# Linear attention block on one core: the five Wk blocks dealt out anew over the two DMA issue queues

## Chip, core and metric

The kernel runs on one core of a Trainium2 chip. The metric is the device time of one execution in microseconds (us); lower is better. The median of the four runs of the kernel before is the reference time.

## What is computed

`x` is [1, 2048, 640], `wqkv` is [640, 1920], `wo` is [640, 640], all bf16. The block is a linear attention with 32 heads of 20 columns:

```
q, k, v = split(x @ wqkv)                 # 3 x [2048, 640], 32 heads of 20
phi(t)  = where(t > 0, t + 1, exp(t)) + 1e-6
kv  = einsum("bhsd,bhse->bhde", phi(k), v)
z   = einsum("bhsd->bhd",       phi(k))
num = einsum("bhqd,bhde->bhqe", phi(q), kv)
den = einsum("bhqd,bhd->bhq",   phi(q), z) + 1e-6
out = (num / den) @ wo
```

## The kernel before, in words

The 2048 rows of `x` are cut into 16 tiles of 128 rows. The contraction over the 640 input columns is cut into five blocks of 128, so the weight for K, `Wk` (columns 640 to 1279 of `wqkv`), is loaded as five blocks of 128 x 640, called Wk blocks 0 to 4 here, 160 KB each.

The program is written as one list of operations for each engine. A helper, `Plan.add`, appends an operation to its engine's list and works out from the names it reads and writes which semaphores it must wait for. Nothing is reordered: the order in which `add` is called for an engine is the order in which that engine runs. A DMA is issued by the engine on whose list it stands. Two engines issue DMAs here, SyncE (SP) and ScalarE (ACT), and each has a queue of its own.

The start of the kernel is what matters for the change:

1. `load_wk` (L234) puts on the two queues the loads needed first: x tile 0 in two halves of 80 KB (L240, one half on each queue), x tile 1 (L229, on ACT) and the five Wk blocks (L249), dealt out by the two strings in L243. A string such as `w12` is Wk block 1, `x12` is x tile 1.
2. `load_xT` (L185) puts four transposing loads on SP (L187), which bring x tiles 2 to 15 straight into `xT`, transposed on the way by the DMA crossbar. They are called crossbar blocks 1 to 4 here and cover 2, 3, 4 and 5 tiles (256, 384, 512 and 640 rows).
3. `load_rest` (L257) puts the weights for Q and V, plain x tiles and `wo` on SP behind them.

TensorE (PE) begins with dummy matmuls (`warm`, L271). It transposes x tiles 0 and 1 itself (`transpose_x`, L197), as these come in plain form. DVE and ACT copy the two transposed tiles to `xT` (L211, L208). Then K is computed for tiles 0 and 1 block by block, in an order written out by hand, so that each Wk block is used as it lands:

```
order = "t1 k00 k10 k01 k11 k02 k12 k03 k13 k04 k14"
```

Here `k01` is the pair of matmuls (two column halves) of tile 0 with Wk block 1. That makes 20 matmuls at L281. Tiles 2 to 15 follow, 10 matmuls each; tile 2 is the first that needs crossbar block 1, tile 4 needs block 2, tile 7 block 3, tile 11 block 4. Each `k_half` waits for the Wk blocks and the part of `xT` that it reads. After K come the Q tiles (L334), the products of `phi(K)` with x (L308), the small products, the denominators and the output product (L514), interleaved by a second hand-written string; they all follow on PE in one fixed order.

Of the kernel before, what the change touches and what calls it, by code (L numbers as in the profile page):

```python
# [84 lines left out]
def bass_standalone__linear_attn_block__prompt_kernel(nc, x, wqkv, wo, out):  # L85
# [12 lines left out]
    with contextlib.ExitStack() as ctx:  # L98
# [129 lines left out]
        def load_xn(a, b, eng):  # L228
            P.add(eng, lambda e: e.dma_start(  # L229
                xn[:, a * D:b * D].rearrange("p (t n) -> p t n", n=D),  # L230
                x[0, 128 * a:128 * b, :].rearrange("(t p) n -> p t n", p=128)),
                writes=[("xn", t) for t in range(a, b)], dma=True)

        def load_wk():  # L234
            tl = mybir.InstLoadActFuncSet(
                name=nc.get_next_instruction_name(),
                act_func_set_id=ACT_TABLE_SET_LN_EXP, ins=[], outs=[])
            P.add("act", lambda e: e.add_instruction(tl), writes=["table"])
            for eng, lo in (("sp", 0), ("act", HALF)):
                P.add(eng, lambda e, lo=lo: e.dma_start(  # L240
                    xn[:, lo:lo + HALF], x[0, 0:128, lo:lo + HALF]),
                    writes=[("xn", 0, lo)], dma=True)
            for eng, what in (("sp", "w01 w23 w34"), ("act", "x12 w12 w45")):  # L243
                for k in what.split():
                    a, b = int(k[1]), int(k[2])
                    if k[0] == "x":
                        load_xn(a, b, eng)
                    else:
                        P.add(eng, lambda e, a=a, b=b: e.dma_start(  # L249
                            wk[:, a * D:b * D].rearrange("p (c n) -> p c n", n=D),  # L250
                            wqkv[128 * a:128 * b, D:2 * D].rearrange("(c p) n -> p c n", p=128)),
                            writes=[("wk", c) for c in range(a, b)], dma=True)
# [304 lines left out]

        pool_const()
        load_wk()
        load_xT()  # L560
        load_rest()
# [142 lines left out]
```

## Time and profile before

| what | value |
|---|---|
| median of 4 runs | 100.68 us (100.56 to 100.93) |
| the profiled execution: its own time | 100.75 us |
| the profiled execution: span of its instructions | 99.3 us |
| PE busy share of the span | 97% |
| DVE, ACT, POOL busy share | 64%, 45%, 5% |
| moved by DMA | 12.26 MB |
| share of 16 DMA engines, SP's queue (q1) and ACT's queue (q10) | 42.6% and 1.8% |

A line of the profile's groups reads: source line, engine, operation, out<-in by the program's names, shape, count; then busy us, mean ns of one, and the idle time of that engine just before them with what ended it. PE is the matmul, PEld the weight load that precedes each matmul, SPq and ACTq the instructions of the two issuing sequencers. "To landing" is counted from the start of the issuing instruction to the last of the DMA's completion signals. In the table by stretches of time, the DMA share is the mean busy share of the 16 DMA engines; it can be over 1 because packets overlap.

### The profile page before, as it was taken

How to read it: one execution, taken by the hardware profiler on the slowest of the kernel's cores; microseconds unless marked ns; L12 is line 12 of the kernel's file. 1: busy time of each engine (PE TensorE's matmuls, PEld its weight loads, DVE VectorE, ACT ScalarE, POOL GpSimd, SP SyncE). 2: the span in 40 equal slices, each digit the busy share in tenths (PEclk: the TensorE clock that was granted, in tenths of full speed). 3: DMA queues.
4: the chain of work that ended last, by engine and by line, in shares of the span. 5: the costliest groups of instructions: out<-in, count | busy, mean ns of one | idle time of the engine just before them, and what ended most of it. 6: DMA issues, size and time to landing. Idle time of an engine off the chain costs nothing.

```text
span 99.3 us, 1793 instructions
## 1 busy us (share of the span) xinstructions
PE 96.1 (97%) x694; PEld 65.0 (65%) x699; DVE 64.1 (64%) x133; ACT 45.2 (45%) x86; POOL 4.5 (5%) x17
## 2 busy tenths in 40 slices
PE   6999999999999999999999999999999999999992
PEld 2567777777756656655768868766556677777771
DVE  2104998888875999968895200669998409954332
ACT  5115455544524071066644364777855622333321
POOL 6300000000000000000002600000000000000000
DMA  1999999999997000000000024220220324273334
GB/s 46 303 266 217 230 195 193 369 374 363 362 243 149 0 0 0 0 3 3 0 7 0 0 61 115 57 65 0 81 63 0 131 60 116 103 255 107 132 132 132
DMA packets 18372, 12.26 MB, mean 123 GB/s; under 512 B 9917, under 2 KB 18365, under 8 KB 18365
## 3 DMA queue, kind: packets, MB, share of 16 engines
q1 hardware_dynamic: 17645, 11.55, 42.6%
q10 hardware_dynamic: 720, 0.61, 1.8%
q8 instruction: 5, 0.08, 0.3%
q14 instruction: 2, 0.02, 0.1%
HBM read 5.90 MB, written 2.62 MB: 86 GB/s over the span
## 4 chain that ended last, share of the span: by engine, by line
PE 96%; ACT 1%; issue 1%; DVE 0%
PE ps L281 22%; PE ps L514 22%; PE ps L334 21%; PE ps L308 18%; PE ps L621 4%; PE ps L271 3%; PE ps L445 2%; PE ps L424 1%; PE ps L197 1%; ACT w2g L464 1%; PE ps L482 1%; DVE osb L539 0%; PE ps L405 0%
## 5 line engine op out<-in xcount | busy, mean ns | idle before, releaser
L334 PE MATMUL ps<-xT,wqn 128*128 128x512 bf16 x95 | 22.6, 379 | 0.4 <-ACT w2g L464 0.2
L281 PE MATMUL ps<-wk,xT 128*128 128x320 bf16 x160 | 22.4, 303 | 0.0
L514 PE MATMUL ps<-w2p,pq 128*128 128x320 bf16 (+2 forms) x170 | 22.1, 291 | 0.0
L342 ACT ACTIVATE eq<-ps 128x512 bf16<-128x512 f32 x20 | 12.0, 598 | 18.6 <-PE ps L334 18.6
L514 PEld LDWEIGHTS ps<-w2p,pq 128*128 128x128 bf16 x170 | 15.9, 98 | 6.2 <-issue 0.2
L281 PEld LDWEIGHTS ps<-wk,xT 128*128 128x128 bf16 x160 | 15.8, 99 | 6.4 <-DMA wk<-in_wqkv_dram 0.3
L308 PE MATMUL ps<-pk,xn 128*128 128x360 bf16 (+1 forms) x130 | 19.1, 299 | 0.0
L334 PEld LDWEIGHTS ps<-xT,wqn 128*128 128x128 bf16 x100 | 11.6, 118 | 8.1 <-ACT w2g L464 0.2
L294 ACT ACTIVATE ek<-ps 128x640 bf16<-128x640 f32 x16 | 11.2, 704 | 11.3 <-PE ps L281 10.6
L308 PEld LDWEIGHTS ps<-pk,xn 128*128 128x128 bf16 x130 | 12.6, 98 | 5.6
L507 DVE TENSOR_TENSOR pq<-pq,rd 128x512 bf16<-128x512 bf16 x20 | 7.7, 419 | 10.7 <-PE ps L621 7.3
L299 DVE SCALAR_TENSOR_TENSOR pk<-ps,ek 128x640 bf16<-128x640 f32 x16 | 13.2, 825 | 0.6
L536 ACT CAST osb<-ps 128x320 bf16<-128x320 f32 (+1 forms) x17 | 7.0, 414 | 12.8 <-PE ps L514 9.4
L539 DVE CAST osb<-ps 128x320 bf16<-128x320 f32 (+2 forms) x17 | 7.7, 465 | 6.3 <-PE ps L514 6.3
L296 DVE TENSOR_SCALAR ek<-ek 128x640 bf16<-128x640 bf16 x16 | 5.2, 325 | 5.5 <-ACT ek L294 5.4
L355 DVE TENSOR_SCALAR eq<-eq 128x512 bf16<-128x512 bf16 x20 | 5.8, 288 | 2.2 <-ACT eq L342 2.1
L346 ACT ACTIVATE rq<-ps 128x512 bf16<-128x512 f32 x11 | 6.5, 591 | 0.0
L362 DVE SCALAR_TENSOR_TENSOR pq<-ps,eq 128x512 bf16<-128x512 f32 x9 | 6.2, 692 | 0.3
L368 DVE TENSOR_TENSOR za<-pk 128x1280 f32<-128x1280 bf16 x4 | 5.8, 1485 | 0.0
L359 DVE TENSOR_TENSOR pq<-eq,rq 128x512 bf16<-128x512 bf16 x11 | 4.7, 426 | 1.1 <-ACT rq L346 0.8
L621 PE MATMUL ps<-pk,xn 128*128 128x360 bf16 (+1 forms) x30 | 4.9, 299 | 0.0
L368 DVE TENSOR_TENSOR za<-za 128x1280 f32<-128x1280 f32 x3 | 4.5, 1484 | 0.0
(44 smaller groups left out, 43.3 us busy)
## 6 DMA issues: line engine op xcount, KB each, us to landing
out_dram<-osb SPq DMA_DIRECT2D x15, 160.0 KB, 1.8
xn<-in_x_dram SPq DMA_DIRECT2D x2, 640.0 KB, 9.5
xn<-in_x_dram SPq DMA_DIRECT2D x1, 960.0 KB, 7.7
wqn<-in_wqkv_dram SPq DMA_DIRECT2D x1, 800.0 KB, 5.6
wv<-in_wqkv_dram SPq DMA_DIRECT2D x1, 800.0 KB, 12.3
wog<-in_wo_dram SPq DMA_DIRECT2D x1, 750.0 KB, 13.2
w2p<-w2g SPq DMA_DIRECT2D x5, 150.0 KB
rd<-rdc SPq DMA_DIRECT2D x8, 64.0 KB, 2.2
```

The lines of the kernel that those rows point to most:

```text
L281: r = e.matmul(bank(b + h, HALF), xT[:, c * S + 128 * st:c * S + 128 * st + 128], wk[:, c * D + HALF * h:c * D + HALF * (h + 1)], start=(c ...
L294: P.add("act", lambda e: e.activation(fold(t[:, :]), two_banks(b), ACTF.Exp), reads=banks + ["table"], writes=[("ek", st % 3)])
L299: P.add("dve", lambda e: e.scalar_tensor_tensor(fold(pk[:, st * D:(st + 1) * D]), two_banks(b), 0.0, fold(t[:, :]), ALU.max, ALU.add), rea ...
L308: r = e.matmul(bank(d, PW[h]), xn[:, st * D + 128 * d:st * D + 128 * d + 128], pk[:, st * D + PO[h]:st * D + PO[h] + PW[h]], start=(st == ...
L334: r = e.matmul(bank(b), wqn[:, d * D:(d + 1) * D].rearrange("p (q c) -> p c q", c=NC_)[:, c, :], xT[:, d * S + BK * sbk:d * S + BK * (sbk ...
L342: P.add("act", lambda e: e.activation(t[:, :], bank(b), ACTF.Exp), reads=[("bank", b), "table"], writes=[("eq", i)])
L368: P.add("dve", lambda e: e.tensor_tensor(d_ap, a, b, ALU.add), reads=ra + rb, writes=[dst])
L507: P.add("dve", lambda e: e.tensor_tensor(v, v, rd[i][:, BK * h:BK * (h + 1)], ALU.mult), reads=[("rd", i, 2 * h), ("rd", i, 2 * h + 1), (" ...
L514: r = e.matmul(bank(b, hi - lo), pq[:, c * S + 128 * st:c * S + 128 * st + 128], w2p[:, c * D + lo:c * D + hi], start=(c == 0), stop=(c == ...
L536: P.add("act", lambda e: e.copy(osb[j][:, lo:hi], bank(b, hi - lo)), reads=[("bank", b)], writes=keys)
L539: P.add("dve", lambda e: e.tensor_copy(osb[j][:, lo:hi], bank(b, hi - lo)), reads=[("bank", b)], writes=keys)
L621: r = e.matmul(bank(d, PW[h]), xn[:, st * D + 128 * d:st * D + 128 * d + 128], pk[:, st * D + PO[h]:st * D + PO[h] + PW[h]], start=False, ...
```

## The change

One line of `load_wk` is changed. The two strings deal out the same five Wk blocks and x tile 1 differently:

```diff
-            for eng, what in (("sp", "w01 w23 w34"), ("act", "x12 w12 w45")):
+            for eng, what in (("sp", "w01 w12 w34 w45"), ("act", "x12 w23")):
```

| place in queue | SP before | SP after | ACT before | ACT after |
|---|---|---|---|---|
| 1 | half of x tile 0 | half of x tile 0 | half of x tile 0 | half of x tile 0 |
| 2 | Wk block 0 | Wk block 0 | x tile 1 | x tile 1 |
| 3 | Wk block 2 | Wk block 1 | Wk block 1 | Wk block 2 |
| 4 | Wk block 3 | Wk block 3 | Wk block 4 | - |
| 5 | crossbar block 1 | Wk block 4 | | |
| 6 and on | crossbar blocks 2 to 4, the rest | crossbar blocks 1 to 4, the rest | | |

The order of work on PE, DVE and GpSimd is the same in both kernels, and so is what each matmul reads and waits for. On ACT one DMA issue ahead of its first copy is gone; on SP there is one more.

## The prediction

> **What bounds the kernel now.** I read the chain of waits first, to see whose time is the end time.
>
> ```profile
> PE 96%; ACT 1%; issue 1%; DVE 0%
> ...
> 3.54 0.53 PE ps L197 x5
> 4.07 0.43 PE ps L271
> 4.50 0.69 PE ps L197 x5
> 5.19 22.19 PE ps L281 x160
> 27.38 1.52 PE ps L308 x10
> ```
>
> The first line is the page's share of the chain, the others are pieces of the chain in order of time (start, us, what). From 5.19 us on it is TensorE without a break: 160 K matmuls in 22.19 us, then the next stage at once. What delays a K matmul therefore moves the end by the same amount, unless a later stretch has slack on PE. Only two of its later pieces are not PE work (an ACT copy at 57.8 us, the last DVE copy), and both follow PE.
>
> Next, the waits of the first 12 us and the timeline of the start, where the change lies.
>
> ```profile
> PEld ps L281 <- DMA wk<-in_wqkv_dram: 0.3, 1, 0.3
> ```
>
> ```profile
> 1.23 1.37 SPq L249 DMA_DIRECT2D wk<-in_wqkv_dram  x3
> 1.72 0.94 ACTq L249 DMA_DIRECT2D wk<-in_wqkv_dram  x2
> 2.65 12.06 SPq L187 DMA_TRANSPOSE xT<-in_x_dram  x4
> 4.98 9.22 PE L281 MATMUL ps<-wk,xT 128*128 128x320 bf16 x63
> 5.92 8.08 PEld L281 LDWEIGHTS ps<-wk,xT 128*128 128x128 bf16 x60 [0.25 <-DMA wk<-in_wqkv_dram]
> ```
>
> The only DMA wait charged to the K stage is the weight load at 5.92 us, 0.25 us long: the fifth matmul waits for Wk block 1, the third DMA on ACT. The SP line shows that the crossbar blocks go out at 2.65 us, directly behind the third Wk block. The three Wk issues fill 1.23 to 2.60 us, and the trace has their starts at 1.232, 1.693 and 2.167 us and the first crossbar start at 2.645 us: one more issue in front costs 0.48 us of SP.
>
> Third, the landings, from the DMA issues around 2.6 us (last column: us from issue to landing).
>
> ```profile
> wk<-in_wqkv_dram ACTq DMA_DIRECT2D x1, 160.0 KB, 4.7
> xT<-in_x_dram SPq DMA_TRANSPOSE x1, 5.4
> ```
>
> Crossbar block 1 starts at 2.645 us and the trace has its last completion at 8.075 us. The first weight load of tile 2, which needs it, stands at 8.117 us, after 0.092 us idle where its neighbours have 0.038 us. So it was released by this landing. The matmul behind it starts at 8.197 us, 0.136 us after the one before: the steady step, nothing lost. This is the reading that carries the forecast: **crossbar block 1 arrives exactly when it is needed**, and no row of waits shows it, because its wait is too short to be listed.
>
> Last, how busy the DMA engines are while it travels (PE, PEld, DVE, ACT, POOL, granted clock, DMA share, GB/s):
>
> ```profile
> 5.00:5.50 0.50, 0.50 (x4) 0.28 (x3) 0.20 (x1) 0.28 (x1) 0.00 (x0) 1.00 0.97 331
> 5.50:6.00 0.50, 0.50 (x3) 0.23 (x2) 0.00 (x0) 0.20 (x1) 0.00 (x0) 1.00 1.33 313
> 6.00:6.50 0.50, 0.50 (x5) 0.38 (x5) 0.00 (x0) 0.00 (x0) 0.00 (x0) 1.00 1.03 138
> 6.50:7.00 0.50, 0.50 (x6) 0.35 (x5) 0.00 (x0) 0.00 (x0) 0.00 (x0) 1.00 1.20 263
> ```
>
> They have work all the time, but in 6.0 to 6.5 us they move only 138 GB/s. This is the main argument against me: what is queued anyway is not delayed by being issued later.
>
> **Part by part.** All times are of the profiled execution (100.75 us, of which 99.3 us span; 0.07 us above the median of 100.68).
>
> *Wk block 1, from third on ACT to third on SP.* The DMA in that SP place now (block 2) starts at 1.693 and lands at 5.658 us; block 1 now starts at 1.716 and lands at 5.876. Gain in landing: 0.22 us. It is worth less on PE. The fourth matmul starts at 5.780, the fifth at 6.023: 0.243 us apart. Matmuls stand 0.267 us apart before that and 0.136 after it, so PE's rate doubles about here (the granted-clock column says 1.00 throughout and doesn't show this). Without the wait the step would lie between 0.136 and 0.267 us: the edit gains between 0.107 us and nothing. I take 0.05, near the middle. Even that is lost if tile 2 then waits for crossbar block 1.
>
> *Wk block 2, to third on ACT.* It would land where block 1 did, 5.88 us; its weight load stands at 6.433. Covered by 0.55 us of block 0 and 1 matmuls. Nothing. *Wk block 3* keeps its place on SP: lands 6.61, used 6.976. Nothing.
>
> *Wk block 4, from fourth on ACT (2.199 us) to fifth on SP (2.645).* Its landing moves from 6.873 to 7.32 us with the issue; its weight load stands at 7.520 (7.47 if the 0.05 is gained). Still 0.15 us of cover. If it came later, tiles 0 and 1 would end late, but that wait overlaps the next one and adds nothing up to some 0.5 us.
>
> *ACT's queue* ends at 2.17 instead of 2.65 us. ACT's next work is the copy at 4.11 us, which waits for PE. Nothing.
>
> *The four crossbar blocks and all of the SP queue behind them* start 0.48 us later. Block 1: landing 8.075 + 0.48 = 8.555 us, against a need at 8.08 to 8.12: cover zero, **+0.48 us on PE**. What is late next: block 2 lands 10.458, needed 10.780; both move by 0.48, so 0.32 us remain. Blocks 3 and 4 land 13.768 and 18.259, needed at 14.855 and after 20 us: free. The Q weight lands 20.35 and is first used at 28.59; the plain x tiles and the rest have microseconds too: free.
>
> *How sure is +0.48?* No row shows a crossbar load behind four Wk blocks. From below: DMA work ahead of it is the same 1.12 MB (x tiles 0 and 1 and five Wk blocks), only on one queue more than on two. If the 16 engines are the limit, block 1 lands as before or, without Wk block 4 mixed into it, a little sooner: 0. From above: now it lands 8.075 - 6.610 = 1.465 us after Wk block 3, the DMA ahead of it on SP. Behind Wk block 4, landing at 7.32, it would land at 8.785: +0.71. I take 0.48, the shift of the issue, nearest the row that was measured (5.4 us from issue to landing), and keep 0 and 0.71.
>
> Here the row is the DMA share of 0.97 to 1.33 with traffic on both queues. The Trainium skill, "DMA: Bandwidth & Descriptors", section "Issuing engines are not separate DMA queues", says that DMAs from different engines interleave on the same 16 DMA engines and that a second issuing engine saves only issue time. By that rule the load on the engines is untouched by the change; with issue hidden behind the backlog the sum would be 0, with issue exposed +0.48. The same page, "Queues, rings and completion order", says that an engine takes the descriptors of one queue in order, which would put Wk block 4 ahead of every packet of crossbar block 1, where it was beside it; that speaks against the change, and no run here shows it yet.
>
> Sum: 100.75 + 0.48 = 101.23 us for the profiled execution, less its 0.07 above the median: **101.16 us**. The gain of 0.05 doesn't count, since it comes before a wait.
>
> **The rivals.**
>
> *Not slower: the DMA backlog hides the later issue.* Mechanism: the engines are still busy with Wk until about 6.2 us, so a crossbar block issued by 5.2 instead of 4.7 us is ready in time. For it: the DMA share near or over 1 from 2.5 us on; landing times growing from 3.0 us for the first Wk block to 4.7 for the last, a queue that builds up. Against it: 138 GB/s in 6.0 to 6.5 us, a time with room. It decides if block 1 lands by 8.12 us. Price: 0 on the crossbar, 0.05 gained at Wk block 1: 100.63 us.
>
> *Faster: Wk block 1's wait goes wholly and crossbar block 1 lands early.* PE could gain the 0.25 us of wait, if its rate were up already at that time, and the 0.05 us by which tile 2's weight load waited: 100.38 us. It needs a landing before 7.8 us, so a better use of the 138 GB/s stretch, and speaks against the 0.136 to 0.267 bound above.
>
> *Slower still: crossbar block 1 starts only when Wk block 4 is through.* +0.71 as worked out: 101.39 us. For it: on SP the first crossbar block follows its forerunner by 1.465 us, too short to begin much earlier. Against it: the trace shows crossbar packets from 5.2 us on, beside Wk packets.
>
> **How the numbers follow.** +0.48: 0.50. Hidden: 0.30. Slower still: 0.12. Faster: 0.08. A measurement of this kernel can tell about 0.3% (0.30 us) from no change. The first and third case are over it: slower 0.62; hidden is within it: same 0.30; the fast case lies at the bound and counts as faster: 0.08. The likeliest case has its own range of 100.98 (just over the bound) to 101.30 us, a little over the full shift. For 8 in 10 I reach down to the hidden case, 100.60, and up to the slower one, 101.40.
>
> **What would show it.** Right: SP's crossbar issue at 3.1 us; a listed wait of PE or PEld at L281 for `xT` of about 0.4 us near 8.1 us, and everything behind it later by that; the wait for `wk` at 5.9 us gone or shorter. Wrong: crossbar block 1 landing within 0.05 us of 8.08 us, with tile 2 at its old time (hidden); or a wait for Wk block 4 near 7.5 us that is longer than the one for `xT`.

## The result and the profile after

The changed kernel takes 101.11 us (median of 53 runs, 100.74 to 102.98), the kernel before 100.84 us (median of 79 runs, 100.37 to 103.05). The ratio is 1.0024, 95% interval 1.0014 to 1.0033: slower by 0.24%, or 0.24 us. That is surely not zero, and it is below the 0.3% that the prediction took for the bound. The forecast was 101.16 us and +0.48 us.

The two sets of runs do not differ by one constant:

| | fastest | lower quartile | median | upper quartile | 9 in 10 are below |
|---|---|---|---|---|---|
| before | 100.37 | 100.62 | 100.84 | 101.02 | 101.34 |
| after | 100.74 | 100.96 | 101.11 | 101.20 | 101.36 |
| difference | +0.37 | +0.34 | +0.27 | +0.18 | +0.02 |

At the short end the times differ by 0.37 us, at the long end by nothing. So something makes executions of one kernel differ by 1 us, and the change does not simply add to it.

Most of the loss lies outside the work that the profile shows. The record has, for each run, its time and the span of its instructions (to 0.1 us). The span goes from the program's first instruction to SP's last wait, for the landing of the last output; the time outside it is the run's time less the span. It is 1.40 us on average over the 57 runs of the kernel before that stand beside the experiments (1.35 to 1.45) and 1.57 us over 54 runs of the changed kernel (1.52 to 1.62): no overlap. So **some 0.17 of the 0.24 us lie before the first or behind the last instruction of the program**, where TensorE waits for no load. The mean spans are 99.52 against 99.47 us (three runs over 101 us of span left out): 0.05 us longer, with an interval (two standard errors, as for all spans below) of 0.08 either way, which includes zero. Less the 0.17, the last row of the table reads +0.20, +0.17, +0.10, +0.01 and -0.15, so the spans of the changed kernel seem to spread less.

The profiled execution of the changed kernel took 101.32 us, in the upper part of its runs. It is 0.57 us longer than the one before; its span, 99.77 us, is 0.43 us longer, and the time outside it 0.14 us. The first lines of the two pages, before and after:

```profile
span 99.3 us, 1793 instructions
span 99.8 us, 1793 instructions
```

Its timeline of the start:

```profile
1.24 1.84 SPq L249 DMA_DIRECT2D wk<-in_wqkv_dram  x4
...
1.72 0.45 ACTq L249 DMA_DIRECT2D wk<-in_wqkv_dram  x1
...
3.13 11.80 SPq L187 DMA_TRANSPOSE xT<-in_x_dram  x4
...
4.97 9.04 PEld L281 LDWEIGHTS ps<-wk,xT 128*128 128x128 bf16 x61
...
5.08 9.13 PE L281 MATMUL ps<-wk,xT 128*128 128x320 bf16 x60
```

SP has four Wk issues and its first crossbar issue at 3.13 us, 0.48 us later, as forecast. The K matmuls begin at 5.08 instead of 4.98 us, and the weight loads run on from 4.97 us in one group with no wait in brackets: the 0.25 us for Wk block 1 is gone. But the wait for crossbar block 1 that the prediction asked for is not there either. Of TensorE's waits for DMA in the first 14 us only this is left:

```profile
PEld ps L197 <- DMA xn<-in_x_dram: 1.3, 2, 0.7
```

The landing of crossbar block 1, from its DMA issue (last column: us from issue to landing):

```profile
xT<-in_x_dram SPq DMA_TRANSPOSE x1, 5.1
```

It was 5.4 before. Issued at 3.126 us, the block landed at 8.214, only 0.14 us later than before. The stretches of 5 to 7 us (columns as above, the last two are DMA share and GB/s) suggest why:

```profile
5.00:5.50 0.50, 0.50 (x5) 0.38 (x4) 0.29 (x1) 0.18 (x1) 0.00 (x0) 1.00 1.06 376
5.50:6.00 0.50, 0.50 (x4) 0.27 (x2) 0.00 (x0) 0.30 (x1) 0.00 (x0) 1.00 1.14 301
6.00:6.50 0.50, 0.50 (x4) 0.27 (x3) 0.00 (x0) 0.00 (x0) 0.00 (x0) 1.00 1.25 239
6.50:7.00 0.50, 0.50 (x5) 0.31 (x4) 0.00 (x0) 0.00 (x0) 0.00 (x0) 1.00 1.28 285
```

In 6.0 to 6.5 us the DMA engines moved 239 GB/s, where they moved 138 before: the poor stretch is better used. In it Wk block 4, from the other queue, was still landing beside the first crossbar packets (6.87 us); now it goes ahead on the same queue and has landed by 6.38. The last experiment shows what such a mix can cost.

What then made the span of this execution longer? Tile 2 begins at 8.615 us against 8.197, and that is TensorE's own pace. Its first six steps between K matmuls are 0.267 us and the seventh 0.170; before, they were three of 0.267 and one of 0.243. All others are 0.136. The 20 matmuls take 3.54 us instead of 3.22, and the 0.10 us by which x tile 1 landed later (4.529 against 4.426) comes on top: 0.42 us. The counts in the rows above say the same: four matmuls in 6.0 to 6.5 us where the kernel before had five. TensorE's rate doubled at about 6.7 us instead of 5.9. From tile 2 on the two profiles are alike: 91.16 and 91.15 us to the end.

### The profile page after: what moved, and what is told of

Same layout as the page of the kernel before. It is cut to its first block, busy times and chain, and to the rows that moved or that the text cites. A ratio compares the mean times of both kernels' runs of the same rounds, so it can differ in the third digit from the quotient of the medians.

```text
span 99.8 us, 1793 instructions
## 1 busy us (share of the span) xinstructions
PE 96.5 (97%) x694; PEld 65.1 (65%) x699; DVE 64.1 (64%) x133; ACT 45.2 (45%) x86; POOL 4.5 (5%) x17
## 4 chain that ended last, share of the span: by engine, by line
PE 92%; DMA 3%; ACT 1%; issue 1%; DVE 0%
PE ps L281 23%; PE ps L514 22%; PE ps L334 21%; PE ps L308 18%; PE ps L621 4%; DMA xn<-in_x_dram 3%; PE ps L445 2%; PE ps L424 1%; ACT w2g L464 1%; PE ps L197 1%; PE ps L482 1%; ACT L238 0%; DVE osb L539 0%; PE ps L405 0%
```

## The experiments

From tile 2's first matmul to the end, six of the seven kernels profiled with their loads at the plain start take 91.1 to 91.2 us; the last one below takes 92.8. So the profiles are read by when tile 2 starts and what it waited for last. The diffs are against the kernel before and show only the strings or lines that differ.

**Theory A**, the forecast's: crossbar block 1 sets tile 2's start and its later issue is the cost. **Theory B**, from the profile after: the cost lies ahead of tile 2, on TensorE. Four kernels on one chip tell them apart, beside 35 runs of the kernel before (median 100.83, fastest 100.43, lower quartile 100.76).

**Only Wk blocks 1 and 2 exchanged**

```diff
-("sp", "w01 w23 w34"), ("act", "x12 w12 w45")
+("sp", "w01 w12 w34"), ("act", "x12 w23 w45")
```

> Wk blocks 1 and 2 exchange queues, Wk block 4 stays on ScalarE, so crossbar block 1 is issued at 2.65 us as in the kernel before. Theory A (crossbar block 1 sets the start of tile 2 whenever TensorE is early, and its later issue is the whole cost of the change): no loss, a ratio of 0.999 to 1.001. Theory B (the cost lies ahead of tile 2 on TensorE: x tile 1 landing 0.10 us later and the doubling of its rate 0.8 us later, as in the profile after): the exchange is what is left to cause it, ratio near 1.002.

Measured: 100.63 us (100.35 to 101.39), ratio 0.9982 with an interval of 0.9958 to 1.0007: no loss shown, and no gain; the 1.002 of theory B is outside the interval. In the profile TensorE was early, and the waits for DMA are these:

```profile
PEld ps L281 <- DMA wk<-in_wqkv_dram: 0.5, 1, 0.5
...
PEld ps L281 <- DMA xT<-in_x_dram: 0.2, 1, 0.2
```

With the rate doubled before the first K matmul, Wk block 1 (landing at 5.80 us) and then crossbar block 1 (8.02 us) hold TensorE, and tile 2 starts at 8.07. A matmul that waited this way starts 0.05 us after the landing.

**Only Wk block 4 moved to SP**

```diff
-("sp", "w01 w23 w34"), ("act", "x12 w12 w45")
+("sp", "w01 w23 w34 w45"), ("act", "x12 w12")
```

> Wk block 4 alone goes to SyncE ahead of the crossbar blocks; Wk blocks 1 and 2 stay where they were before. Crossbar block 1 is issued 0.48 us later. Theory A: the whole loss of the change, ratio 1.002 to 1.004. Theory B: no loss, 0.999 to 1.001.

Measured: median 101.05 us, all 12 runs within 100.80 to 101.14; the ratio of 0.9997 (0.9985 to 1.0010) shows neither gain nor loss, and the 1.002 to 1.004 of theory A is outside its interval. The plain means, 101.01 against 100.89 us, do lie 0.12 us apart, and no run is in the lowest quarter of the kernel before, and none at its upper end. The profile, tile 2 at 8.356 us, has another limit than theory A's:

```profile
6.17 7.86 PEld L281 LDWEIGHTS ps<-wk,xT 128*128 128x128 bf16 x59 [0.82 <-DMA wk<-in_wqkv_dram]
```

Wk block 1, third on ACT, landed at 6.13 us here; 16 matmuls at 0.136 us follow, while crossbar block 1 had landed by 7.98. It was issued as late as in the changed kernel and came 0.1 us earlier than in the kernel before.

**A small DMA ahead of the crossbar blocks**

```diff
+dum = sb("dum", 8)
...
+P.add("sp", lambda e: e.dma_start(dum[:, :], wo[0:128, 0:8]), writes=["dum"], dma=True)
 load_xT()
```

> The kernel before with one more DMA on SyncE ahead of the crossbar blocks, which loads 2 KB (128 rows of 16 bytes) that nothing uses. Issue of the crossbar blocks comes about 0.45 us later, while the DMA engines get hardly more to move. Theory A with issue as the limit: block 1 lands 0.45 us later and the kernel loses 0.3 to 0.45 us, ratio 1.003 to 1.0045. Theory A with the backlog as the limit (what counts is what is queued ahead): landing within 0.1 us of before, ratio 0.999 to 1.001. Theory B: 0.999 to 1.001.

Measured: 100.86 us, ratio 1.0004 (0.9983 to 1.0025). So 0.48 us of SP issue time by itself costs less than 0.25%, and a loss of 0.3 us or more, as from a landing bound to the issue, is outside the interval. The profile is of its slowest run (101.48 us), in which all early landings were late, x tile 1 by 0.5 us, so its 8.76 us for crossbar block 1 is no measure of the issue.

**All five Wk blocks on SP**

```diff
-("sp", "w01 w23 w34"), ("act", "x12 w12 w45")
+("sp", "w01 w12 w23 w34 w45"), ("act", "x12")
```

> All five Wk blocks on SyncE ahead of the crossbar blocks, ScalarE issues only half of x tile 0 and x tile 1. Crossbar block 1 is issued about 0.96 us later than before, twice the shift of the change. Theory A with issue as the limit: landing near 8.9 to 9.0 us, a loss of 0.7 to 0.9 us, ratio 1.007 to 1.009. With the backlog as the limit: the same bytes are ahead of it as in the change, landing near 8.2 us, ratio 1.002 to 1.004. Theory B: no loss from the crossbar blocks; Wk blocks 3 and 4 come a little later, below 0.2 us.

Measured: 101.43 us, ratio 1.0050 (1.0031 to 1.0070), twice the loss of the change; its fastest run is 0.56 us above the fastest of before. The profile:

```profile
3.60 11.56 SPq L187 DMA_TRANSPOSE xT<-in_x_dram  x4
...
5.45 2.29 PEld L281 LDWEIGHTS ps<-wk,xT 128*128 128x128 bf16 x18 [0.28 <-DVE xT L211]
...
8.56 5.41 PEld L281 LDWEIGHTS ps<-wk,xT 128*128 128x128 bf16 x41 [0.83 <-DMA xT<-in_x_dram]
```

This is the wait that the prediction described, 0.83 us long: the weights load through all 20 matmuls of tiles 0 and 1 without waiting for Wk, then stop until crossbar block 1 is there (8.52 us). An issue 0.95 us later moved the landing by 0.45 us. Here the mechanism of theory A is seen at work, with half of the shift. Theory B doesn't explain it: TensorE was early in this execution, which is the fastest of the twelve.

**TensorE made early: four kernels whose loads start late.** To take the doubling of the rate out, the first load on each queue waited for 12 dummy matmuls:

```diff
 pool_const()
+warm(12)
+start = P.ops["pe"][-1]
 load_wk()          # first load on each queue: after=[start]
...
-warm(6)
+warm(11)
```

> The kernel before, but the first load on either queue waits until TensorE has done 12 dummy matmuls, and 11 more cover the time until x tile 0 is there. By then TensorE should run at its full step (0.136 us for a 128 x 320 matmul) in every execution. It is the base for the three kernels beside it, about 5 us slower than the kernel without this. Theory A: tile 2 starts on the landing of crossbar block 1 or on Wk block 1, whichever is later. If the rate's doubling is what spreads the times, these runs spread less than the 1 us of the kernel before; if DMA landings spread them, as much.

> The changed kernel with the same late start of the loads. Theory A: 0.3 to 0.45 us slower than the base beside it, the shift that the fast ends of the plain kernels show (100.37 against 100.74 us), with TensorE waiting for crossbar block 1 before tile 2. Theory B (the loss lies ahead of tile 2, in x tile 1 and the doubling of the rate): within 0.1 us of the base, since nothing is left to double late.

> The same late start with Wk blocks 1 and 2 exchanged and Wk block 4 left on ScalarE. Theory A: 0 to 0.15 us faster than the base: Wk block 1 comes some 0.1 to 0.2 us earlier and crossbar block 1 as before. Theory B: as the base.

> The same late start with Wk block 4 alone moved to SyncE. Theory A: the whole loss, 0.3 to 0.45 us slower than the base, crossbar block 1 the last to land before tile 2. If instead Wk block 1 on ScalarE sets the start of tile 2, as in the profile of the plain kernel with Wk block 4 moved, the loss is below 0.2 us and the wait before tile 2 is not listed.

Measured: 106.07, 106.08, 105.90 and 105.83 us; with six runs each and intervals of about 0.4% either way they tell nothing apart. The hope of less spread failed: the 12 dummy matmuls last as long as TensorE's rate lets them, so the loads themselves started at different times (the first at 5.89 us with block 4 alone, at 6.12 to 6.13 us in the other three profiles), and the base took 105.11 to 106.29 us. The profiles are of use, though. In all four TensorE is early and waits for crossbar block 1; in the base and in the changed kernel:

```profile
13.63 0.39 PEld L281 LDWEIGHTS ps<-wk,xT 128*128 128x128 bf16 x4 [0.55 <-DMA xT<-in_x_dram]
```

```profile
13.69 0.39 PEld L281 LDWEIGHTS ps<-wk,xT 128*128 128x128 bf16 x4 [0.47 <-DMA xT<-in_x_dram]
```

With TensorE early, the crossbar block binds in both kernels. Counted from the first load's issue it lands at 7.45 us in the base, 7.53 in the changed kernel, 7.45 with the exchange alone and 7.33 with block 4 alone.

**Theory C** came out of these: tile 2 starts on the latest of TensorE's own pace, Wk block 1 and crossbar block 1, and which of them is last changes from profile to profile. One execution of each kernel was profiled; that it also changes between executions of one kernel is argued, not shown. Its rival is that the backlog hides the later issue altogether.

**The same with a fixed delay.** A chain of DVE memsets held the loads back instead, with 20 dummy matmuls:

```diff
+for _ in range(14):
+    P.add("dve", lambda e: e.memset(dly[:, :], 0.0), writes=["dly"], after=P.ops["dve"][-1:])
+start = P.ops["dve"][-1]
 load_wk()          # first load on each queue: after=[start]
...
-warm(6)
+warm(20)
```

> The kernel before, its loads held back by a chain of 14 DVE memsets (about 5 us, a fixed time), with 20 dummy matmuls, so that TensorE runs at its full step before the first K matmul, and the start of the loads does not hang on TensorE's rate as it did with the wait on dummy matmuls. Base of the two beside it, some 5 us slower than the plain kernel. If the doubling of the rate makes the plain kernel's spread of 1 us, these runs spread less than 0.5 us.

> The changed kernel, held back in the same way. Theory C (tile 2 starts on the latest of TensorE's own pace, Wk block 1 and crossbar block 1; with TensorE early the later crossbar block is the price): 0.1 to 0.4 us slower than the base. Rival (the DMA backlog hides the later issue: crossbar block 1 landed 7.45 us after the first load's issue in the base with dummy matmuls and 7.53 us in the changed one): within 0.1 us of the base, and then the loss of the plain kernel needs another cause.

> Only Wk blocks 1 and 2 exchanged, held back in the same way. Theory C: 0 to 0.15 us faster than the base. Rival: as the base.

Measured: ratios 1.0766 (1.0717 to 1.0814), 1.0792 (1.0752 to 1.0832) and 1.0802 (1.0753 to 1.0851): undecided. The control missed its aim. The chain took until 7.86 us, TensorE had nothing to do for 3.4 us before x tile 0 (in the base), and its rate fell back. From the stretches of the base (the column before the DMA share is the granted clock):

```profile
10.00:11.00 1.00, 0.67 (x6) 0.34 (x6) 0.29 (x1) 0.21 (x1) 0.00 (x0) 1.00 0.94 282
11.00:12.00 1.00, 0.11 (x2) 0.12 (x3) 0.00 (x0) 0.26 (x1) 0.00 (x0) 0.58 0.97 341
12.00:13.00 1.00, 1.00 (x8) 0.77 (x8) 0.29 (x1) 0.36 (x1) 0.00 (x0) 0.50 1.07 354
```

So these three measure TensorE at half clock, not the crossbar. Their landings of block 1, from the first load's issue: 7.03, 8.11 and 7.70 us.

**The other direction: crossbar block 1 one place earlier**

```diff
-("sp", "w01 w23 w34"), ("act", "x12 w12 w45")
+("sp", "w01 w12"), ("act", "x12 w23 w34 w45")
```

> Without any holding back: Wk blocks 0 and 1 on SyncE, then the crossbar blocks; x tile 1 and Wk blocks 2, 3 and 4 on ScalarE. Crossbar block 1 is issued at 2.17 us, 0.48 us earlier than in the kernel before, and Wk block 4 at 2.7 us on ScalarE. Theory C: crossbar block 1 is off the limit, gain up to 0.2 us, unless Wk block 4, now sharing the engines with crossbar packets, lands after 7.4 us and makes TensorE wait before tile 2 (then a listed wait for wk, and no gain). Rival (issue time hidden by the backlog): same as before within 0.1 us.

Measured: 104.10 us, ratio 1.0265 (1.0206 to 1.0324). Neither theory had this. The profiled execution is one of the longer ones (104.64 us; the shortest took 102.92). The granted clock over the whole run is 0.98 in the three longest and 1.00 in the others, which still lose some 2 us and more; no profile shows one of those. Its timeline, then its stretches:

```profile
2.17 14.22 SPq L187 DMA_TRANSPOSE xT<-in_x_dram  x4
...
10.01 3.94 PEld L281 LDWEIGHTS ps<-wk,xT 128*128 128x128 bf16 x19 [2.56 <-DMA wk<-in_wqkv_dram]
```

```profile
7.00:8.00 1.00, 0.79 (x6) 0.34 (x4) 0.00 (x0) 0.00 (x0) 0.00 (x0) 1.00 1.28 148
8.00:9.00 1.00, 0.00 (x0) 0.00 (x0) 0.00 (x0) 0.00 (x0) 0.00 (x0) 1.00 1.38 131
9.00:10.00 1.00, 0.00 (x0) 0.00 (x0) 0.00 (x0) 0.00 (x0) 0.00 (x0) 1.00 1.27 136
...
11.00:12.00 1.00, 1.00 (x6) 0.54 (x5) 0.73 (x2) 0.79 (x2) 0.00 (x0) 0.50 1.00 191
```

Wk block 4, issued 0.5 us after the first crossbar block, landed at 9.97 us, 7.3 us after its issue, and the crossbar block, issued 0.48 us earlier than before, at 10.17, 2.1 us later. While both were in flight the DMA engines were busy (1.27 to 1.38) and moved 131 to 148 GB/s. TensorE then waited 2.56 us, and 0.8 us after the wait its granted clock fell to 0.50 for some 3.4 us.

**What the spans of these runs add**

| kernel | DMAs on SP between x tile 0 and the crossbar | runs | outside the span, us | mean span, us |
|---|---|---|---|---|
| before | 3 | 57 | 1.40 | 99.47 |
| only blocks 1 and 2 exchanged | 3 | 12 | 1.39 | 99.37 |
| changed | 4 | 54 | 1.57 | 99.52 |
| only block 4 moved to SP | 4 | 12 | 1.57 | 99.44 |
| a small DMA more | 4 | 12 | 1.56 | 99.37 |
| all five blocks on SP | 5 | 12 | 1.27 | 100.14 |
| crossbar one place earlier | 2 | 6 | 1.28 | 102.63 |

The mean spans leave out the same three runs as above. The 0.17 us outside the span come with a fourth DMA there, even one of 2 KB, and not with the exchange of blocks 1 and 2. The seven kernels with held loads show the same: 1.40 to 1.41 us with three, 1.56 to 1.58 us with four. With two or five it is shorter than with three, so it does not grow with the count; what happens in this time, and why it changes, no run shows.

Within the span, against the 35 runs of the kernel before on the same chip (mean 99.50 us), the exchange alone is 0.13 us shorter (interval 0.21 either way), block 4 alone 0.06 us shorter (0.10), the small DMA 0.13 us shorter (0.18). None of the three differs clearly from zero, block 4 alone and the small DMA with the crossbar's issue 0.48 us later. The five blocks on SP do lengthen the span, by 0.64 us (0.17 either way); the ratio shows less, as 0.13 us are gained outside it.

## Why the prediction was right or wrong

- **The time and direction were right, the mechanism was not, and the close hit is in part luck.** +0.48 us was put on crossbar block 1; the runs lost 0.24 us, and some 0.17 us of that lie outside the span of the instructions, where the prediction had no term: it took what lies outside the 99.3 us of span as fixed. Within the span 0.05 to 0.07 us are left, which the runs can't tell from zero. The forecast of 101.16 us lies 0.05 us from the measured median because the median of the kernel before came out at 100.84 us, not the 100.68 us of the four runs that it started from.
- **The crossbar term.** Block 1's landing moved by 0.14 us in the profiled pair (8.075 to 8.214), not 0.48. Over eleven profiles (all but those of the small DMA, the five blocks and the earlier crossbar), from the first load's issue, block 1 lands at 7.03 to 7.70 us (mean 7.36 of six) where it goes out 1.87 us after that issue, and at 7.19 to 8.11 (mean 7.52 of five) where it goes out 2.34 us after it. The mean shift of 0.16 us is smaller than the scatter, and without the three kernels with the fixed delay it is 0.01 us; most of the issue's 0.48 us is hidden. This is the hidden rival's mechanism, given 0.30 and priced at nothing for the crossbar. The upper bound of +0.71 found no support.
- **"Cover zero" was wrong by 0.08 us.** I read the matmul 0.12 us behind the landing as its shortest way. After a real wait it starts 0.05 us behind it, so the block could have landed at 8.15 us without loss.
- **Where it binds, it costs as described.** With TensorE early, block 1 sets tile 2's start in both kernels (0.55 and 0.47 us of wait with held loads), and with twice the shift the spans grow by 0.64 us with a listed wait of 0.83 us. That this is also the 0.20 us that remain at the short end of the times is argued from these; no profile shows the changed kernel in one of its shortest executions.
- **TensorE's doubling** was taken as fixed at 5.9 us. In the profiles with the loads at the plain start it comes between 3.8 us (the exchange alone) and 6.7 us (after). Where it comes late, as in the profile after, TensorE is the last to be ready and the crossbar block is free. The wait of about 0.4 us that the prediction asked for isn't in that profile; tile 2 is nearly as late as forecast (0.42 us) for this other reason.
- **Wk block 1** landed 0.37 us earlier (5.50 against 5.88), its wait went, as forecast. When TensorE is early the wait is larger than the profile of before showed (0.5 to 0.8 us in two kernels). In the exchange alone Wk block 1 and the crossbar block limit within 0.1 us of each other; with block 4 alone Wk block 1 limits by 0.3 us.
- **Wk block 4** landed at 6.38 us, not 7.32; it kept its cover and more. Blocks 2 and 3, ACT's queue and the later crossbar blocks show no wait in the profile after, as forecast.
- **The rule weighed.** The Trainium skill's "DMA: Bandwidth & Descriptors", section "Issuing engines are not separate DMA queues", says that DMAs issued by different engines run on the same 16 DMA engines and interleave there. The landings agree: with the same loads ahead of it, 0.48 us of later issue moved the crossbar block by 0.14 us. The profiled pair hints that the mix in flight counts too: 138 against 239 GB/s in 6.0 to 6.5 us.

What stays open: what the time outside the span holds, and why it is 0.17 us longer with one more DMA on SP; whether the change costs anything within the span; and why executions of one kernel differ by 1 us. The move of Wk block 4 carries the 0.17 us, since the exchange alone does not have it.

## What to carry to other kernels

Before a small difference is put down to a wait, split each run's time into the span of its instructions and the rest: here 0.17 of 0.24 us were in the rest, where no wait for a load can be. When several events end within 0.1 us of each other, one profile shows whichever came last in that execution; compare the whole distribution of runs. A later issue need not be a later landing while the DMA engines have a backlog (0.48 us moved it by 0.14 us, 0.95 us by 0.45); ask what is in flight together. In this kernel a plain load issued just behind a crossbar transpose came 3 us later, and all five loads ahead of it on its queue cost time as well.

## What was not expected of the hardware

- TensorE's first doubling of rate varied from 3.8 to 6.7 us with the same dummy work ahead of it, and the granted-clock column said 1.00 all the while; it shows a later fall (0.50 after 3.4 us without work, and after a wait of 2.56 us), but not the slow start.
- A plain load of 160 KB issued just behind a crossbar transpose took 7.3 us to land instead of 4.7, and the transpose 8.0 instead of 5.4 (one profile).
- The time of a run outside the span of its instructions is constant for each kernel within about 0.06 us either way, rounding included, and it moved by 0.17 us with one more DMA on SP.
